# Re-pacing loads, crossbar transposes and attention units in a fused attention and bilinear feed-forward kernel

## The chip, the cores and the metric

The kernel runs on one core of a Trainium2 chip. The metric is the device time of one execution in microseconds (us). The profile's span, from the first to the last instruction, is about 2 us shorter. TensorE does the matrix products, ScalarE (ACT) and VectorE (DVE) empty the accumulators, GpSimd (POOL) copies, and issues the loads from memory. The SyncE queue (SPq) issues crossbar transposes and stores.

## The reference

For each of 4 batches and 8 heads, the sequence of 768 is cut into 8 blocks of 96. A Sinkhorn-normalised 8x8 matrix P mixes the blocks of k and v; attention is taken inside each block; and the result goes through a bilinear feed-forward network.

```python
k_sorted = einsum('bhij,bhjcd->bhicd', P, k_blocks)      # v likewise
attn     = softmax(scale * q_blocks @ k_sorted^T)         # inside each block
x        = (attn @ v_sorted)  as  [4*768, 512]
out      = ((x @ w_a) * (x @ w_b)) @ w_out                # 512 -> 1536 -> 512
```

## The kernel before

Heads are taken in pairs: batch 0 has pairs 0 to 3, batch 1 has 4 to 7, and so on. While TensorE computes the feed-forward products of batch b, the attention "units" of batch b+1 are put in between the products. A pair has three units: mix (k and v by P), scores (q times k, then exp), and o (weights times v). Three values per pair go through a crossbar transpose on the SyncE queue: q (tile `qTf`), mixed v (tile `vs`), and the o stage's result (`xp` to `xT`). `xT` is what the next batch's products read.

```python
def c_(g):                      # mix unit of pair g
    if g == HP: stage_q(g)
    if g + 1 < B * HP: stage_q(g + 1)          # transpose of a later q
    if g + 2 < B * HP: pair_q(g + 2)           # GpSimd copy ahead of it
    if g + HP < B * HP: load_pair((g + HP) // HP, g % HP)   # loads, one batch ahead
    stage_mix(g, "k", ("act",))
    stage_mix(g, "v", ("dve", "act"))          # ends in the transpose to vs
def o_(g):
    stage_o(g)                                 # o_ps <- vs, eT ; xp on DVE
    to_xT(g)                                   # transpose xp -> xT
# units of a batch: c4, sc4, c5, o4, sc5, c6, o5, sc6, c7, o6, sc7, o7
# interleave: one unit every so many steps; a step is a product pair (ffn_ab) or an output product (ffn_out)
...
# before batch 1 starts, on the GpSimd queue:
for hp in range(2): load_pair(1, hp)           # two pairs of batch 1
spread(nc.gpsimd, p_col, 8, 8)                 # 2 us
for c in range(3): load_out(c)                 # w_out
pair_q(HP); pair_q(HP + 1)
for hp in range(2, HP): load_pair(1, hp)       # the other two pairs
```

In the profile, `pf` and `two` are the accumulators of ffn_ab (x times w_a or w_b), and `po` that of ffn_out (one step is 12 matmuls). `mix`, `sc` and `o_ps` are the units.

The softmax here doesn't subtract the row's maximum and nothing guards it: scores larger than these inputs give would overflow.

Of the kernel before, what the change touches and what calls it, by code (L numbers as in the profile page):

```python
# [10 lines left out]
BF16 = mybir.dt.bfloat16  # L11
# [5 lines left out]
def _ap(t: bass.AP, extra_offset, pattern):  # L17
    return bass.AP(tensor=t.tensor, offset=t.offset + extra_offset,
                   ap=[list(p) for p in pattern])
# [3 lines left out]
def kernel(  # L23
# [11 lines left out]
    nc = tc.nc  # L35
    P = 128
    B, H, S, D = q.shape
    NB = sort_net.shape[-1]
# [7 lines left out]
    NCH = S // P  # L46
    HP = H // 2
    KA = DMODEL // P
    KO = DFF // P
# [11 lines left out]
    const = ctx.enter_context(tc.tile_pool(name="const", bufs=1))  # L61
    ld = ctx.enter_context(tc.tile_pool(name="ld", bufs=8))
    qtp = ctx.enter_context(tc.tile_pool(name="qtp", bufs=5))
# [23 lines left out]
    def load_pair(b, hp):  # L87
        tiles = []
        for name, t in (("k2", k), ("v2", v), ("q2", q)):
            base = (b * H + 2 * hp) * S * D  # L90
            if b == 0 and name == "q2":
                continue
            to = ld.tile([P, 2, W], BF16, tag=name, name=name)
            nc.gpsimd.dma_start(out=to, in_=_ap(t, base, [[W, P], [S * D, 2], [1, W]]))  # L94
            tiles.append(to)
        loaded[b * HP + hp] = tiles
# [43 lines left out]
    st = {}  # L140
    xTs = {}

    def xT_of(b):
        if b not in xTs:
            xTs[b] = xtp.tile([P, KA, S], BF16, tag="xT", name="xT")
        return xTs[b]

    s_all = const.tile([P, BH, NB, CG], BF16, name="s_all")
    p_col = const.tile([P, NB, BH], BF16, name="p_col")

# [7 lines left out]
    def copy(eng, out, in_):  # L158
        if eng == "act":
            nc.scalar.copy(out=out, in_=in_)  # L160
        else:
            nc.vector.tensor_copy(out=out, in_=in_)  # L162
# [89 lines left out]


    def pair_q(g):
        qc = qtp.tile([P, NCH, 2, D], BF16, tag="qc", name="qc", bufs=3)
        nc.gpsimd.tensor_copy(out=qc.rearrange("p c e d -> p e c d"),  # L256
                              in_=loaded[g][2].rearrange("p e (c d) -> p e c d", c=NCH))
        st[g, "qc"] = qc

    def stage_q(g):  # L260
        qT = qtp.tile([P, NCH, P], BF16, tag="qTf", name="qTf", bufs=3)
        nc.sync.dma_start_transpose(out=qT, in_=st[g, "qc"].rearrange("p c e d -> p (c e d)"))
        st[g, "qT"] = qT

# [21 lines left out]
    def stage_scores(g):  # L286
        kT, qT, eT = kTs[g % NBUF], st[g, "qT"], eTs[g % NBUF]
        for hf in range(2):
            sc = psA.tile([P, 2, 512], FP32, tag="A", name="sc")
            for i in range(NBH):  # L290
                for e in range(2):
                    blk = hf * NBH + i
                    nc.tensor.matmul(  # L293
                        sc[:, e, i * BLK:(i + 1) * BLK],
                        lhsT=kT[e * D:(e + 1) * D, blk * BLK:blk * BLK + P],
                        rhs=qT[e * D:(e + 1) * D, :, blk * CG:(blk + 1) * CG],
                        start=True, stop=True)
            nc.scalar.activation(out=eT[:, hf, :, 0:HB], in_=sc[0:BLK, :, 0:HB],  # L298
                                 func=AF.Exp, scale=float(scale))
# [7 lines left out]
    def to_xT(g):  # L307
        xT, xp = xT_of(g // HP), st[g, "xp"]
        nc.sync.dma_start_transpose(
            out=xT[:, g % HP, :].rearrange("p (i t) -> p i t", i=NB),  # L310
            in_=xp.rearrange("p i e d -> p (i e d)"))
# [9 lines left out]
    def ab_mms(pf, w_sb, b, m, t, kcs):  # L321
        for kc in kcs:
            nc.tensor.matmul(pf[:, 0:HW], lhsT=w_sb[:, kc, m * P:(m + 1) * P],  # L323
                             rhs=x_cols(b, kc, t), start=(kc == 0), stop=(kc == KA - 1))

    def hT_of(b):
        if b not in hTs:
            hTs[b] = ffp.tile([P, KO, S], BF16, tag="hT", name="hT")
        return hTs[b]

    def ffn_ab(b, m, t, begun=()):
        hT = hT_of(b)
        ab = []
        for n, w_sb in enumerate((w_a_sb, w_b_sb)):
            if n < len(begun):
                pf, k0 = begun[n], KA - 1
            else:
                pf, k0 = psF.tile([P, 512], FP32, tag="F", name="pf"), 0
            ab_mms(pf, w_sb, b, m, t, range(k0, KA))
            ab.append(pf)  # L340
            if n == 0:
                a_sb = ffp.tile([P, HW], BF16, tag="a_sb", name="a_sb", bufs=4)
                nc.scalar.copy(out=a_sb, in_=pf[:, 0:HW])  # L343
        nc.vector.tensor_mul(out=hT[:, m, t * HW:(t + 1) * HW], in0=a_sb,  # L344
                             in1=ab[1][:, 0:HW])

    def ffn_out(b, c):
        hT = hTs[b]
        po = psF.tile([P, DMODEL], FP32, tag="F", name="po")
        for m in range(KO):  # L350
            nc.tensor.matmul(po, lhsT=hT[:, m, c * P:(c + 1) * P], rhs=w_out_sb[:, m, :],  # L351
                             start=(m == 0), stop=(m == KO - 1))
        o_sb = ffp.tile([P, DMODEL], FP32, tag="o_sb", name="o_sb", bufs=3)
        copy("act" if c % 2 == 0 else "dve", o_sb, po)
        if b == 0:
            h, u = divmod(c, 3)
            for c2 in range(2):
                nc.sync.dma_start(
                    out=_ap(out, (h * PH * NCH + 2 * u + c2) * DMODEL,
                            [[NCH * DMODEL, PH], [1, DMODEL]]),  # L360
                    in_=o_sb[c2 * PH:(c2 + 1) * PH])
        else:
            rows = out[b * S:(b + 1) * S, :].rearrange("(p c) n -> c p n", c=NCH)
            nc.sync.dma_start(out=rows[c], in_=o_sb)


    with tc.manual_schedule(engines={ET.PE, ET.Pool, ET.SP}):
        with tc.manual_schedule(engines={ET.Activation, ET.DVE}):
# [4 lines left out]
            for it in range(5):  # L373
                nc.scalar.activation(out=p_nat, in_=p_nat, func=AF.Exp)  # L374
                if it == 2:
                    with nc.allow_low_precision("sum of one one and zeros"):
                        nc.vector.reduce_sum(
                            out=mask, in_=_ap(ident, 0, [[P, P], [1, CG], [CG, NB]]),
# [10 lines left out]
                else:  # L389
                    nc.vector.tensor_mul(  # L390
                        out=p_fin.bitcast(BF16).rearrange("h (i j u) -> h i j u", i=NB, j=NB),
# [69 lines left out]

        for c in range(4, 6):
            load_ab(c)
        for hp in range(2):
            load_pair(1, hp)
        spread(nc.gpsimd, p_col, 8, 8)
        for c in range(3):
            load_out(c)
        pair_q(HP)
        pair_q(HP + 1)  # L470
        for hp in range(2, HP):
            load_pair(1, hp)
        for g in range(2, 4):
            spread(nc.gpsimd, p_col, g * 8, 8)

# [25 lines left out]
        def units_full(b):  # L501
            g0, us = b * HP, []

            def c_(g):
                if g == HP:
                    stage_q(g)
                if g + 1 < B * HP:
                    stage_q(g + 1)
                if g + 2 < B * HP:
                    pair_q(g + 2)  # L510
                if g + HP < B * HP:
                    load_pair((g + HP) // HP, g % HP)
                stage_mix(g, "k", ("act",))
                stage_mix(g, "v", ("dve", "act"))

            def o_(g):
                stage_o(g)
                to_xT(g)

            for n in range(HP + 1):  # L520
                if n < HP:
                    us.append(lambda g=g0 + n: c_(g))
                if n > 0:
                    us.append(lambda g=g0 + n - 1: o_(g))
                if n < HP:
                    us.append(lambda g=g0 + n: stage_scores(g))
            return us

        def interleave(steps, units, spare, slow=0):
            n, done = len(steps), 0  # L530
            for s, step in enumerate(steps):
                step()
                want = s + 1 if s < slow else -(-(s + 1) * len(units) // (n - spare))
                while done < min(want, len(units)):
                    units[done]()
                    done += 1

        steps = [lambda: ffn_ab(0, 0, 0, begun[0:2]), lambda: ffn_ab(0, 1, 0, begun[2:4]),
                 lambda: ffn_ab(0, 2, 0, begun[4:5])]
        steps += [lambda m=m: ffn_ab(0, m, 0) for m in range(3, KO)]  # L540
        interleave(steps, units_half(), 1, 3)

        steps = [lambda m=m: ffn_ab(0, m, 1) for m in range(KO)]
        steps += [lambda c=c: ffn_out(0, c) for c in range(NCH)]
        interleave(steps, units_full(1), 2)

        for b in range(1, B):
            steps = [lambda m=m, t=t, b=b: ffn_ab(b, m, t)
                     for m in range(KO) for t in range(2)]
            steps += [lambda c=c, b=b: ffn_out(b, c) for c in range(NCH)]  # L550
            interleave(steps, units_full(b + 1) if b + 1 < B else [], 2)


# [28 lines left out]
```

## Time and profile before

| before | value |
|---|---|
| time, median | 256.2 us (3 runs, 253.7 to 257.0) |
| span of the profiled run | 252.7 us |
| TensorE busy | 234.4 us |
| mean granted TensorE clock | 0.993 |
| TensorE waits for transposes | 5.4 us |

The page's first part has, for each engine, busy microseconds, share of the span, and instruction count.

```profile
PE 234.4 (93%) x2219; PEld 135.6 (54%) x2229; DVE 108.2 (43%) x259; ACT 102.4 (41%) x202; POOL 61.4 (24%) x83
```

TensorE is idle for 18.3 us. The list of TensorE's waits (who waited for what: total us, times, longest) says what can be removed.

```profile
PE q_ps L175 <- DMA q_first<-in_q_dram: 6.2, 1, 6.2
PE o_ps L241 <- DMA vs<-vT: 5.4, 2, 3.3
PE o_ps L241 <- ACT eT L210: 0.6, 1, 0.6
```

The first line is the start. The second is two waits for a transposed v. The table of stretches (window and length, then busy time of each engine, then the granted clock, DMA share and GB/s) shows that everything removable is in one stretch, the time of batch 0's second half beside batch 1's attention.

```profile
45.00:92.70 47.70, 42.01 (x397) 23.30 (x399) 17.27 (x37) 18.63 (x36) 20.49 (x26) 0.96 1.36 180
92.70:147.40 54.70, 54.60 (x489) 31.42 (x489) 23.10 (x47) 23.91 (x47) 7.47 (x10) 1.00 0.59 108
147.40:202.00 54.60, 54.49 (x488) 31.50 (x489) 23.06 (x47) 23.91 (x47) 0.00 (x0) 1.00 0.34 74
```

The timeline of TensorE (start, length, instruction, count; in brackets the idle time before it and what ended it) shows the second wait and its cost afterwards.

```profile
76.44 1.04 PE L241 MATMUL o_ps<-vs,eT 96*128 96x65 bf16 x16 [3.33 <-DMA vs<-vT]
77.29 4.02 PE L351 MATMUL po<-w_out_sb,hT 128*128 128x512 bf16 x12
81.25 0.52 PE L293 MATMUL sc<-qTf,kT 64*128 64x96 bf16 x16
81.69 2.76 PE L351 MATMUL po<-w_out_sb,hT 128*128 128x512 bf16 x11
```

Twelve matmuls take 4.02 us right after the idle time; eleven take 2.76 us a little later. The granted clock between 77.5 and 79.5 us is 0.50.

Why is v late? The view of DMA issues gives us from issue to landing. The first line here is the v transpose issued at 63.4 us, in the crowded stretch; the second is the transpose to xT issued at 129.8 us, with no load beside it.

```profile
vs<-vT SPq DMA_TRANSPOSE x1, 12.9
xT<-xp SPq DMA_TRANSPOSE x1, 2.8
```

### The profile page before, as it was taken

The page shows a single profiled execution, that of the slowest core. Times are in us where ns is not written, and L with a number is a line of the kernel's source. Part 1 is how long each engine was busy: PE and PEld are TensorE (multiplying, and loading weights), DVE is VectorE, ACT ScalarE, POOL GpSimd, SP SyncE. Part 2 cuts the span into 40 slices and gives each one's busy share as a digit, 9 for nine tenths or more (in the row PEclk, how much of TensorE's full clock was granted, in tenths as well). Part 3 has the DMA queues.
Part 4 walks back from the last instruction along what each step waited for, and adds up shares of the span by engine and source line. Part 5 has one row for each costly group of instructions (what it writes and reads, how often), then busy time and mean ns, then how long its engine had stood idle before and what let it go on. Part 6 is the DMA issues. An engine that isn't in the chain of part 4 may idle for free.

```text
span 252.7 us, 5448 instructions
## 1 busy us (share of the span) xinstructions
PE 234.4 (93%) x2219; PEld 135.6 (54%) x2229; DVE 108.2 (43%) x259; ACT 102.4 (41%) x202; POOL 61.4 (24%) x83
## 2 busy tenths in 40 slices
PE   0999899969958999999999999999999999999993
PEld 0475566536624455666654456666654466665441
DVE  6775456535613313555453133645533144444111
ACT  3385555556520217463740137465440033333010
POOL 8974678554715305300100000000000000000000
PEclk9999999999997999999999999999999999999999
DMA  6999999999999998992332343332244210000122
GB/s 88 197 199 196 197 200 201 190 169 184 146 129 199 239 204 160 160 116 45 72 65 83 115 118 73 67 74 40 42 35 125 113 44 0 0 0 4 52 114 83
DMA packets 56441, 28.67 MB, mean 113 GB/s; under 512 B 33376, under 2 KB 53344, under 8 KB 56416
## 3 DMA queue, kind: packets, MB, share of 16 engines
q0 software_dynamic: 20944, 14.16, 40.6%
q1 hardware_dynamic: 35472, 14.17, 28.9%
q8 instruction: 17, 0.28, 0.4%
q14 instruction: 8, 0.07, 0.1%
HBM read 28.32 MB, written 6.29 MB: 137 GB/s over the span
## 4 chain that ended last, share of the span: by engine, by line
PE 83%; DMA 9%; DVE 5%; ACT 1%; issue 1%; DVEq 0%
PE pf L323 46%; PE po L351 24%; DMA vs<-vT 8%; PE o_ps L241 3%; PE mix L272 3%; PE sc L293 2%; PE mixh L191 2%; PE vs_ps L218 1%; PE sc L206 1%; PE xt_ps L232 1%; DMA p_nat<-in_sort_net_dram 1%; DVE hT L344 1%; DVE xph L247 1%; DVE csum L384 1%; ACT p_nat L374 1%
## 5 line engine op out<-in xcount | busy, mean ns | idle before, releaser
L344 DVE TENSOR_TENSOR hT<-a_sb,pf 128x384 bf16<-128x384 bf16 x95 | 52.6, 554 | 74.0 <-PE pf L323 45.5
L323 PE MATMUL pf<-xT,w_a_sb 128*128 128x384 bf16 x380 | 78.1, 327 | 0.0
L323 PE MATMUL pf<-xT,w_b_sb 128*128 128x384 bf16 x380 | 77.5, 326 | 0.0
L343 ACT CAST a_sb<-pf 128x384 bf16<-128x384 f32 x95 | 45.5, 479 | 65.9 <-PE pf L323 49.4
L351 PE MATMUL po<-w_out_sb,hT 128*128 128x512 bf16 x279 | 64.5, 385 | 0.5
L323 PEld LDWEIGHTS <-w_b_sb 128*128 128x128 bf16 x384 | 37.5, 98 | 25.1 <-issue 0.6
L323 PEld LDWEIGHTS <-w_a_sb 128*128 128x128 bf16 x384 | 34.6, 98 | 22.1
L351 PEld LDWEIGHTS <-hT 128*128 128x128 bf16 x288 | 28.0, 99 | 33.3 <-issue 1.6
L162 DVE COPY o_sb<-po 128x512 f32<-128x512 f32 x12 | 8.3, 692 | 47.8 <-PE po L351 31.3
L160 ACT COPY o_sb<-po 128x512 f32<-128x512 f32 x12 | 7.0, 586 | 43.0 <-PE po L351 23.1
L298 ACT ACTIVATE eT<-sc 96x768 bf16<-96x768 f32 x24 | 18.1, 802 | 12.4 <-PE sc L293 12.4
L256 POOL COPY qc<-q 128x768 bf16<-128x768 bf16 x12 | 9.9, 826 | 53.1 <-DMA qTf<-qc 34.0
L241 PE MATMUL o_ps<-vs,eT 96*128 96x65 bf16 x256 | 11.6, 196 | 6.1 <-DMA vs<-vT 5.4
L247 DVE TENSOR_TENSOR xp<-o_ps,rec 96x512 bf16<-96x512 f32 x24 | 15.5, 680 | 0.3
L241 PEld LDWEIGHTS <-eT 96*128 96x128 bf16 x256 | 10.5, 99 | 8.9 <-issue 6.3
L160 ACT CAST kT<-mix 128x384 bf16<-128x384 f32 x24 | 10.3, 482 | 6.2 <-PE mix L272 6.2
L94 POOL DMA_DIRECT2D v<-in_v_dram x16 | 11.5, 718 | 1.8 <-DMA w_b_sb<-in_moe_w_b_dram 0.8
L94 POOL DMA_DIRECT2D k<-in_k_dram x16 | 11.5, 719 | 1.2 <-DMA w_a_sb<-in_moe_w_a_dram 0.6
L245 DVE RECIPROCAL rec<-o_ps 96x8 f32<-96x8 f32 x32 | 5.2, 185 | 12.1 <-PE o_ps L241 12.0
L94 POOL DMA_DIRECT2D q<-in_q_dram x12 | 8.6, 719 | 1.3 <-DMA w_a_sb<-in_moe_w_a_dram 0.7
L175 PE MATMUL q_ps<-ident,q_first 64*64 64x64 bf16 x96 | 3.0, 217 | 6.2 <-DMA q_first<-in_q_dram 6.2
L210 ACT ACTIVATE eT<-sc 96x768 bf16<-96x768 f32 x8 | 6.5, 808 | 2.5 <-PE sc L206 2.5
(69 smaller groups left out, 138.4 us busy)
## 6 DMA issues: line engine op xcount, KB each, us to landing
out_dram<-o_sb SPq DMA_DIRECT2D x18, 256.0 KB, 2.0
k<-in_k_dram POOLq DMA_DIRECT2D x16, 192.0 KB, 6.4
v<-in_v_dram POOLq DMA_DIRECT2D x16, 192.0 KB, 6.8
q<-in_q_dram POOLq DMA_DIRECT2D x12, 192.0 KB, 9.1
w_a_sb<-in_moe_w_a_dram POOLq DMA_DIRECT2D x6, 256.0 KB, 10.8
w_b_sb<-in_moe_w_b_dram POOLq DMA_DIRECT2D x6, 256.0 KB, 10.7
w_out_sb<-in_moe_w_out_dram POOLq DMA_DIRECT2D x3, 512.0 KB, 10.9
out_dram<-o_sb SPq DMA_DIRECT2D x12, 128.0 KB, 5.1
```

Of the source, the lines that this page charges most:

```text
L94: nc.gpsimd.dma_start(out=to, in_=_ap(t, base, [[W, P], [S * D, 2], [1, W]]))
L160: nc.scalar.copy(out=out, in_=in_)
L162: nc.vector.tensor_copy(out=out, in_=in_)
L241: nc.tensor.matmul(o_ps[:, e, i * (D + 1):(i + 1) * (D + 1)], lhsT=eT[:, hf, e, i * BLK:i * BLK + P], rhs=vs[0:BLK, i0 + i, V0 - 1 + e * ( ...
L247: nc.vector.tensor_tensor(out=_ap(xp, i0 * 2 * D, [[nxp * 2 * D, BLK], [D, 2], [2 * D, NBH], [1, D]]), in0=_ap(o_ps, 1, [[1024, BLK], [511 ...
L256: nc.gpsimd.tensor_copy(out=qc.rearrange("p c e d -> p e c d"), in_=loaded[g][2].rearrange("p e (c d) -> p e c d", c=NCH))
L272: nc.tensor.matmul(mix[e * D:(e + 1) * D, c // 3, c % 3 * P:(c % 3 + 1) * P], lhsT=src2[:, e, c * D:(c + 1) * D], rhs=s_all[:, 2 * g + e], ...
L298: nc.scalar.activation(out=eT[:, hf, :, 0:HB], in_=sc[0:BLK, :, 0:HB], func=AF.Exp, scale=float(scale))
L323: nc.tensor.matmul(pf[:, 0:HW], lhsT=w_sb[:, kc, m * P:(m + 1) * P], rhs=x_cols(b, kc, t), start=(kc == 0), stop=(kc == KA - 1))
L343: nc.scalar.copy(out=a_sb, in_=pf[:, 0:HW])
L344: nc.vector.tensor_mul(out=hT[:, m, t * HW:(t + 1) * HW], in0=a_sb, in1=ab[1][:, 0:HW])
L351: nc.tensor.matmul(po, lhsT=hT[:, m, c * P:(c + 1) * P], rhs=w_out_sb[:, m, :], start=(m == 0), stop=(m == KO - 1))
```

## The change

The intent is to keep loads out of the way of transposes and to give each transpose more time. It has three parts:

- **L**, load order. All of batch 1's loads are issued first, then w_out, then all four q copies and their transposes.
- **G**, gate. A later batch's loads move from the mix unit to the o stage, after a one-element GpSimd copy that reads the o stage's result `xp`. So GpSimd can't issue them before that o stage is done. The later q copies and transposes move with them.
- **U**, units. The order becomes mix, scores, o of the pair before, so a v transpose has five units' time instead of four. Units are spread by TensorE time, an ffn_out step counting as two ffn_ab steps.

```diff
 # L
-        for hp in range(2):
+        for hp in range(HP):
             load_pair(1, hp)
         spread(nc.gpsimd, p_col, 8, 8)
         for c in range(3):
             load_out(c)
-        pair_q(HP)
-        pair_q(HP + 1)
-        for hp in range(2, HP):
-            load_pair(1, hp)
+        for g in range(HP, 2 * HP):
+            pair_q(g)
+            stage_q(g)
 # G
             def c_(g):
-                ... stage_q(g + 1), pair_q(g + 2), load_pair((g + HP) // HP, g % HP)
                 stage_mix(g, "k", ("act",))
                 stage_mix(g, "v", ("dve", "act"))
             def o_(g):
                 stage_o(g)
                 to_xT(g)
+                if 2 * HP <= g + 2 < B * HP:
+                    pair_q(g + 2)
+                    stage_q(g + 2)
+                if g + HP < B * HP:
+                    nc.gpsimd.tensor_copy(out=gate, in_=st[g, "xp"][0:1, NB - 1, 1, D - 1:D])
+                    load_pair((g + HP) // HP, g % HP)
 # U
                 if n < HP:
                     us.append(lambda g=g0 + n: c_(g))
+                    us.append(lambda g=g0 + n: stage_scores(g))
                 if n > 0:
                     us.append(lambda g=g0 + n - 1: o_(g))
-                if n < HP:
-                    us.append(lambda g=g0 + n: stage_scores(g))
+        def paced(ab, po, units, spare):
+            steps = [(1, f) for f in ab] + [(2, f) for f in po]
+            total = sum(t for t, f in steps) - 2 * spare
+            ...                       # runs a unit while done * total < now * len(units)
 # cuts: the two q tiles get 4 buffers instead of 3; the calls of interleave are replaced
```

After the last o stage two ffn_out steps are left in batch 0 and three in the others; it was three and four.

More of the change, by code (lines that the diff above doesn't have):

```diff
@@ L146, in xT_of @@
         return xTs[b]
+    gate = const.tile([1, 1], BF16, name="gate")
     s_all = const.tile([P, BH, NB, CG], BF16, name="s_all")
@@ L254, in pair_q @@
     def pair_q(g):
-        qc = qtp.tile([P, NCH, 2, D], BF16, tag="qc", name="qc", bufs=3)
+        qc = qtp.tile([P, NCH, 2, D], BF16, tag="qc", name="qc", bufs=4)
         nc.gpsimd.tensor_copy(out=qc.rearrange("p c e d -> p e c d"),
@@ L260, in stage_q @@
     def stage_q(g):
-        qT = qtp.tile([P, NCH, P], BF16, tag="qTf", name="qTf", bufs=3)
+        qT = qtp.tile([P, NCH, P], BF16, tag="qTf", name="qTf", bufs=4)
         nc.sync.dma_start_transpose(out=qT, in_=st[g, "qc"].rearrange("p c e d -> p (c e d)"))
@@ L504, in c_ @@
             def c_(g):
-                if g == HP:
-                    stage_q(g)
-                if g + 1 < B * HP:
-                    stage_q(g + 1)
-                if g + 2 < B * HP:
-                    pair_q(g + 2)
-                if g + HP < B * HP:
-                    load_pair((g + HP) // HP, g % HP)
                 stage_mix(g, "k", ("act",))
@@ L536, in interleave @@
                     done += 1
+        def paced(ab, po, units, spare):
+            steps = [(1, f) for f in ab] + [(2, f) for f in po]
+            total = sum(t for t, f in steps) - 2 * spare
+            now = done = 0
+            for t, step in steps:
+                step()
+                now += t
+                while done < len(units) and done * total < now * len(units):
+                    units[done]()
+                    done += 1
         steps = [lambda: ffn_ab(0, 0, 0, begun[0:2]), lambda: ffn_ab(0, 1, 0, begun[2:4]),
@@ L541 @@
         interleave(steps, units_half(), 1, 3)
-        steps = [lambda m=m: ffn_ab(0, m, 1) for m in range(KO)]
-        steps += [lambda c=c: ffn_out(0, c) for c in range(NCH)]
-        interleave(steps, units_full(1), 2)
-        for b in range(1, B):
-            steps = [lambda m=m, t=t, b=b: ffn_ab(b, m, t)
-                     for m in range(KO) for t in range(2)]
-            steps += [lambda c=c, b=b: ffn_out(b, c) for c in range(NCH)]
-            interleave(steps, units_full(b + 1) if b + 1 < B else [], 2)
+        for b in range(B):
+            ab = [lambda m=m, t=t, b=b: ffn_ab(b, m, t)
+                  for m in range(KO) for t in range(2) if b > 0 or t == 1]
+            po = [lambda c=c, b=b: ffn_out(b, c) for c in range(NCH)]
+            paced(ab, po, units_full(b + 1) if b + 1 < B else [], 2)
 _INS = ['q', 'k', 'v', 'sort_net', 'moe_w_a', 'moe_w_b', 'moe_w_out']
```

## The prediction

> **What bounds it now.** TensorE: 234.4 of 252.7 us busy (page, part 1). In the table of stretches it is idle 0.1 of 46.8 us in 92.7-139.5 and 0.1 of 46.6 us in 147.4-194: nothing to gain there. Of its 18.3 us idle, 6.2 are the start and 4 the tail, both untouched; the rest stands between 45 and 77 us: the list of waits shows two TensorE waits for the crossbar-transposed v (o_ps for vs), 2.12 us at 57.1 and 3.33 us at 76.4, 5.45 us together. After the second the granted clock is 0.50 until about 80 us: the next 12 po matmuls take 4.02 us instead of 2.65, o_ps 1.04 instead of 0.65, 1.76 us more. This fits the Trainium skill, "TensorE: Matmul & The Clock Gate", Part 1, where an idle window of about 3.4 us halves the clock; the 2.12 us stall left it at 1.00. Removable: about 7.2 us.
>
> **Why the stalls.** Transposes that land in 2.8-3.3 us in the quieter stage (94-130 us) take 7.6-12.9 us in 49-77 us (DMA view), beside loads of batch 1 issued at 39.8-43.2 and of batch 2 at 53-70. The vs that stalls longest: issued 63.4, landed 76.3. The skill's "DMA: Bandwidth & Descriptors", "Issuing engines are not separate DMA queues", says all issuers share 16 engines and interleave; the trace agrees.
>
> **What changes.** TensorE executes the same instructions, reordered. Batch 1's twelve loads are issued together, w_out after them, then four pair_q copies (0.82 us each) and their transposes. Loads of batch 2 start only after the first full o stage (about 60 us instead of 53). A vs gets five units instead of four: in this stage about 9-11 us instead of 7. Both old stalls should go: -7 us.
>
> **What comes back.**
> 1. The first full pair's q transpose was issued at 36.9 and landed 9.7 us later, at 46.6, before its scores at 49.5. Now it stands behind six more loads, a 2.0 us spread and w_out on GpSimd: issued at about 43, with some 8 us of loads still queued, landing at about 51-53. Estimate: a new stall of 2 us (0-4).
> 2. Batch 1's last o stage is followed by 2 po (5.3 us) instead of 3 (7.9). Before, the last xT landed 8.2 us after that stage and only just sufficed. Loads gated by the preceding o stage collide with it. Estimate: 1.5 us (0-4) before batch 1's first product finishes, at kc = 3.
> 3. Later batches keep three po there: nothing.
>
> Sum: -7.2 +2 +1.5 = -3.7 us on a median of 256.2: **252.5 us**, range 248.7 to 256.2. Faster by over 2%: 0.34; within 2%: 0.62; slower by over 2%: 0.04.
>
> **What would show it.** Right: no o_ps wait for vs; vs landings of 3-6 us in 50-85 us; clock 1.0 at 77-80 us; TensorE busy about 232.5 us; first batch-2 load at about 60 us. The first scores waiting for qTf near 50 us, and the product after the last po of batch 0 waiting for xT near 90 us, would show items 1 and 2.
>
> **What would make it wrong.** If the q transposes overtake the queued loads and xT lands sooner without them, all 7 us come through: 249, faster. If the first vs queues behind four q transposes until past its o stage (about 60 us), or a new stall is long enough to halve the clock again, the gain is gone: 255-256.

## The result, and the profile after

| | before | after |
|---|---|---|
| time, median | 256.6 us (4 runs, 253.7 to 262.2) | 270.5 us (4 runs, 269.3 to 271.4) |
| span, profiled run | 252.7 | 268.1 |
| TensorE busy | 234.4 | 237.9 |
| mean granted clock | 0.993 | 0.967 |

The ratio is 1.058, with a 95% interval of 1.047 to 1.069. Ratios here are the mean time of one kernel's fast runs over that of the other's fast runs of the same rounds, so they are not quite the ratio of the medians. The runs of before vary between rounds and chips (medians of 256.3 to 259.6 us), so kernels are compared by ratio.

The change made the kernel 5.8% slower; 1.4% faster was predicted (252.5 on 256.2). The page's first part, after:

```profile
PE 237.9 (89%) x2217; PEld 137.3 (51%) x2229; DVE 109.2 (41%) x259; ACT 102.5 (38%) x202; POOL 63.1 (24%) x91
```

TensorE's idle time grew from 18.3 to 30.2 us (268.1 - 237.9), and its busy time by 3.5 us for the same matmuls. Those two make up the whole 15.4 us of span. The list of waits names the idle time:

```profile
PE pf L324 <- DMA xT<-xp: 10.6, 2, 6.4
PE sc L294 <- DMA qTf<-qc: 5.7, 2, 4.7
PE o_ps L242 <- DMA vs<-vT: 0.2, 1, 0.2
```

The old waits for v are gone, as intended. In their place products wait for xT at the starts of batches 1 and 2, and scores wait for q. The timeline of TensorE shows the three longest and the slow clock after each:

```profile
55.05 0.83 PE L294 MATMUL sc<-qTf,kT 64*128 64x96 bf16 x16 [4.68 <-DMA qTf<-qc]
55.81 1.46 PE L324 MATMUL pf<-xT,w_a_sb 128*128 128x384 bf16 x4
...
99.79 0.48 PE L324 MATMUL pf<-xT,w_a_sb 128*128 128x384 bf16 x1 [6.37 <-DMA xT<-xp]
100.06 1.48 PE L324 MATMUL pf<-xT,w_b_sb 128*128 128x384 bf16 x4
...
161.56 0.40 PE L324 MATMUL pf<-xT,w_a_sb 128*128 128x384 bf16 x1 [4.20 <-DMA xT<-xp]
161.75 1.49 PE L324 MATMUL pf<-xT,w_b_sb 128*128 128x384 bf16 x4
...
165.48 0.81 PE L324 MATMUL pf<-xT,w_b_sb 128*128 128x384 bf16 x4
```

Four pf matmuls take 0.81 us at full clock, and 1.46 to 1.49 us after a stall. The table of stretches shows the cost by place; the two short rows are the starts of batches 1 and 2.

```profile
45.00:93.40 48.40, 43.13 (x405) 24.04 (x408) 18.12 (x39) 18.75 (x36) 15.66 (x21) 0.93 0.90 131
93.40:104.00 10.60, 4.23 (x35) 2.41 (x34) 1.43 (x3) 1.74 (x4) 0.82 (x1) 0.68 1.13 191
104.00:157.30 53.30, 52.08 (x453) 29.85 (x455) 21.73 (x45) 22.17 (x44) 11.67 (x19) 1.00 0.66 94
157.30:166.00 8.70, 4.50 (x38) 2.60 (x37) 1.78 (x3) 2.05 (x5) 1.64 (x2) 0.80 0.85 187
166.00:217.20 51.20, 51.04 (x448) 29.33 (x450) 21.72 (x44) 21.82 (x43) 0.00 (x0) 1.00 0.30 70
```

Why is xT late? First the SyncE queue and then GpSimd, at the end of batch 0 (same columns as the timeline). The transpose of 89.94 us is the one that TensorE waits for until 99.79.

```profile
85.86 1.24 SPq L310 DMA_TRANSPOSE xT<-xp  x1
87.20 1.36 SPq L263 DMA_TRANSPOSE qTf<-qc  x1
88.65 1.20 SPq L359 DMA_DIRECT2D out_dram<-o_sb  x2
89.94 2.02 SPq L310 DMA_TRANSPOSE xT<-xp  x1
```

```profile
85.96 0.18 POOL L515 COPY gate<-xp 1x1 bf16<-1x1 bf16 x1 [5.91 <-DVE xp L248]
86.47 0.72 POOL L94 DMA_DIRECT2D k<-in_k_dram  x1 [0.34 <-issue]
...
90.14 0.18 POOL L515 COPY gate<-xp 1x1 bf16<-1x1 bf16 x1
90.27 0.72 POOL L94 DMA_DIRECT2D k<-in_k_dram  x1
```

The gate opens when `xp` is written, and the transpose of `xp` is issued at that same moment (85.86 beside 85.96, 89.94 beside 90.14). So each pair's three loads start together with that pair's transpose. At the end of a batch the two last o stages are one ffn_out step apart, so six loads are near the last transpose. It lands after 9.8 us here, and after 9.9 us at the end of batch 1. In the middle of batch 1, where only the three loads of its own stage are beside it, it takes 4.5 to 5.2 us. The view of DMA issues for the transpose of 89.94 us:

```profile
xT<-xp SPq DMA_TRANSPOSE x1, 9.8
```

The first wait is another matter. On GpSimd, the q copies now stand behind six more loads, the spread and w_out. The transpose of the first q is issued at 43.45 us (36.88 before) and lands 11.5 us later (9.7 before), at about 54.9. The SyncE queue, the first line from before and the second from after, and then the landing in after:

```profile
36.88 4.25 SPq L262 DMA_TRANSPOSE qTf<-qc  x2
43.45 11.53 SPq L263 DMA_TRANSPOSE qTf<-qc  x4
```

```profile
qTf<-qc SPq DMA_TRANSPOSE x1, 11.5
```

### The profile page after: what moved, and what is told of

Read it like the earlier page. It is cut to its first block, busy times and chain, and to the rows that moved or that the text cites. A ratio compares the mean times of both kernels' runs of the same rounds, so it can differ in the third digit from the quotient of the medians.

```text
span 268.1 us, 5456 instructions
## 1 busy us (share of the span) xinstructions
PE 237.9 (89%) x2217; PEld 137.3 (51%) x2229; DVE 109.2 (41%) x259; ACT 102.5 (38%) x202; POOL 63.1 (24%) x91
## 4 chain that ended last, share of the span: by engine, by line
PE 64%; DMA 27%; POOL 5%; issue 2%; DVE 1%; SPq 1%; POOLq 0%; DVEq 0%
PE pf L324 39%; PE po L352 18%; DMA xT<-xp 7%; DMA qTf<-qc 7%; DMA w_b_sb<-in_moe_w_b_dram 4%; DMA v<-in_v_dram 4%; PE mix L273 3%; DMA vs<-vT 3%; DMA k<-in_k_dram 2%; PE sc L294 2%; PE o_ps L242 2%; POOL w_out_sb L110 1%; POOL s_all L153 1%; POOL q_first L82 1%; POOL w_a_sb L105 1%
## 5 line engine op out<-in xcount | busy, mean ns | idle before, releaser
L324 PE MATMUL pf<-xT,w_a_sb 128*128 128x384 bf16 x380 | 80.1, 333 | 10.6 <-DMA xT<-xp 10.6
L324 PE MATMUL pf<-xT,w_b_sb 128*128 128x384 bf16 x380 | 79.4, 332 | 0.0
L352 PE MATMUL po<-w_out_sb,hT 128*128 128x512 bf16 x277 | 63.2, 379 | 0.7 <-issue 0.2
L324 PEld LDWEIGHTS <-w_a_sb 128*128 128x128 bf16 x384 | 35.4, 99 | 23.7 <-issue 1.9
L352 PEld LDWEIGHTS <-hT 128*128 128x128 bf16 x288 | 27.4, 98 | 31.4
L299 ACT ACTIVATE eT<-sc 96x768 bf16<-96x768 f32 x24 | 18.1, 803 | 11.3 <-PE sc L294 11.3
L515 POOL COPY gate<-xp 1x1 bf16<-1x1 bf16 x8 | 1.4, 180 | 72.9 <-DVE xp L248 72.9
L94 POOL DMA_DIRECT2D k<-in_k_dram x16 | 11.5, 719 | 4.2 <-issue 1.3
L94 POOL DMA_DIRECT2D v<-in_v_dram x16 | 11.5, 717 | 3.6 <-DMA w_b_sb<-in_moe_w_b_dram 2.0
L294 PE MATMUL sc<-qTf,kT 64*128 64x96 bf16 x192 | 6.5, 210 | 5.7 <-DMA qTf<-qc 5.7
L294 PEld LDWEIGHTS <-kT 64*128 64x128 bf16 x192 | 4.7, 97 | 10.0 <-issue 7.3
```

The lines of the kernel that those rows point to most:

```text
L94: nc.gpsimd.dma_start(out=to, in_=_ap(t, base, [[W, P], [S * D, 2], [1, W]]))
L294: nc.tensor.matmul(sc[:, e, i * BLK:(i + 1) * BLK], lhsT=kT[e * D:(e + 1) * D, blk * BLK:blk * BLK + P], rhs=qT[e * D:(e + 1) * D, :, blk ...
L299: nc.scalar.activation(out=eT[:, hf, :, 0:HB], in_=sc[0:BLK, :, 0:HB], func=AF.Exp, scale=float(scale))
L324: nc.tensor.matmul(pf[:, 0:HW], lhsT=w_sb[:, kc, m * P:(m + 1) * P], rhs=x_cols(b, kc, t), start=(kc == 0), stop=(kc == KA - 1))
L352: nc.tensor.matmul(po, lhsT=hT[:, m, c * P:(c + 1) * P], rhs=w_out_sb[:, m, :], start=(m == 0), stop=(m == KO - 1))
```

## The experiments

Two causes were supposed, each with a rival. For xT: theory A, the gate's collision of loads with the transpose; rival B, that the pacing leaves too few products after the last o stage. For q: theory C, its place on the GpSimd queue; rival D, that transposes are slow there whatever their place. In the kernels with parts switched off, the q tiles keep their four buffers. All runs gave correct results.

| run | parts | wait for qTf | for xT | for vs | median us | ratio to before (95%) |
|---|---|---|---|---|---|---|
| before | none | 0 | 0 | 5.4 | 256.6 | 1 |
| after | L G U | 5.7 | 10.6 | 0.2 | 270.5 | 1.058 (1.047-1.069) |
| e3_LU | L U | 4.8 | 3.5 | 2.2 | 263.3 | 1.031 (1.017-1.046) |
| e6_LG | L G | 5.0 | 0 | 0 | 255.0 | 1.004 (0.992-1.016) |
| e2_GU | G U | 1.0 | 11.4 | 0 | 263.1 | 1.033 (1.016-1.050) |
| e4_U_again | U | 0 | 4.1 * | 6.2 * | 259.3 | 1.011 (1.003-1.018) |
| e5_G | G | 0 | 1.3 | 2.0 | 251.4 | 0.980 (0.971-0.988) |
| e7_LG_qfirst | L G, q first | 0 * | 4.0 * | 3.0 * | 254.5 | 0.995 (0.987-1.004) |
| e10_qfirst | L G U, q first | 0.6 * | 10.6 * | 0 * | 265.5 | 1.038 (1.030-1.046) |
| e11_old_order | L G, pacing of U | 2.1 | 2.2 | 0 | 259.7 | 1.014 (1.004-1.024) |
| e8_after_xT | L G U, last loads late | 5.6 | 0.5 | 0 | 255.8 | 1.002 (0.996-1.008) |
| e9_spare4 | L G U, 4 steps spare | 9.7 | 1.6 | 0 | 266.2 | 1.040 (1.032-1.047) |
| e12_both | L G U, both mends | 1.0 | 0.5 | 0 | 249.5 | 0.976 (0.970-0.983) |

Waits are those of the profiled run of each. A star marks a profile that fell in a slow run (over 1.5% above that kernel's fastest), so its waits are not an example of the fast runs.

### Parts switched off

**e3_LU**: without the gate.

```diff
 def c_(g):
+    if g + 1 >= 2 * HP and g + 1 < B * HP: stage_q(g + 1)
+    if g + 2 >= 2 * HP and g + 2 < B * HP: pair_q(g + 2)
+    if g + HP < B * HP: load_pair((g + HP) // HP, g % HP)
 def o_(g):
-    pair_q(g + 2); stage_q(g + 2); gate; load_pair(...)
```

> The changed kernel with its gate taken out: loads of later batches and the later q copies stand in the mix unit again, ungated, as before the change; load order and pacing stay new. Theory A (the gate releases a pair's loads at the moment its xT transpose is issued, so they share the DMA engines): the two waits of the product for xT (6.4 and 4.2 us in the changed kernel) go, with their slow-clock tails, 14 us less, about 256 us; the first scores still wait about 4.7 us for qTf. Rival B (pacing leaves too few products after the last o stage): the xT waits stay near 10 us and the time near 268 us.

The xT waits fell from 10.6 to 3.5 us, both parts of it now at the start of batch 1. At the end of batch 1 the last xT lands in 2.8 us, and there is no wait. But 256 us did not come: the time was 263.3. The 3.5 us for xT stayed, the ungated loads brought back a wait of 2.2 us for v, and the mean clock was still 0.974. Theory A holds for the start of batch 2. At the start of batch 1 the last xT took 7.5 us beside ungated loads. Before, one that took 6.6 us with one more product after it cost no wait, so the new pacing has a part in this one.

**e6_LG**: the old unit order and spread.

```diff
-    c_(n), stage_scores(n), o_(n-1)      # paced
+    c_(n), o_(n-1), stage_scores(n)      # interleave(ab + po, units, 2)
```

> The changed kernel with the old unit order and the old even spread over steps; load order and gate stay new. Theory A: xT waits remain at both batch starts, smaller by the one more product of 2.6 us that follows the last o stage: about 3.5 and 1.5 us instead of 6.4 and 4.2; total 262 to 266 us. Rival B: both xT waits under 0.5 us, total about 256 us. Under both the first scores still wait for qTf.

The xT waits are gone, which is what rival B said and theory A did not. The last xT of batch 1 lands in 4.7 us instead of 9.9, with the gate still there. So the gate alone does not do it; gate and unit order do it together. (The old spread also leaves one more product at the end; e11 below takes that out.) That is a third theory, E: the two last o stages stand one step apart and release their loads nearly at once.

**e2_GU**: the old load order.

```diff
-for hp in range(HP): load_pair(1, hp)
+for hp in range(2): load_pair(1, hp)
 spread; w_out
-four pair_q and stage_q
+pair_q(HP); pair_q(HP + 1); the other two pairs of loads   # stage_q in the mix units
```

> The changed kernel with the old initial order: two pairs of batch 1, w_out, two q copies and then the other two pairs. Theory C (the first q transposes come late because six more loads and w_out stand before them on the GpSimd queue): the wait of the first scores for qTf falls from 4.7 us to under 0.5 us, its slow-clock tail of 2 us goes, and the total is about 6.8 us less, 263.5 us; xT waits stay about 10 us. Rival D (the transposes are slow there whatever their place, because w_out or the loads fill the DMA engines): the wait stays over 2 us.

As theory C expected: the first scores no longer wait, and the time fell to 263.1 us (263.5 expected). The 1.0 us left is at 122.2 us, at scores of batch 2.

**e4_U** and **e4_U_again**: the kernel before with unit order and pacing alone (the diff's part U).

> The kernel before with only the new unit order and pacing (five units instead of four between a v transpose and its o stage); loads as before the change. If the old stalls come from too short a lead, the o_ps wait for vs falls from 5.45 us to under 3 us; xT waits at the start of batch 1 at most 3 us (one product fewer after the last o stage), none at the start of batch 2. Theory A: 252 to 256 us. Rival B: xT waits of about 10 us in all, over 262 us.

The profiled execution of e4_U took 1336 us, and its other three runs 256.8 to 262.4, so the ratio was unclear. In that one execution the products' matmuls were over four times as long (pf 1.35 to 1.38 us on average instead of 0.33, po 1.70 instead of 0.39), though the recorded mean clock was 1.0; VectorE and ScalarE kept theirs (0.55 us for the product into hT, 0.48 for the copy of pf). It says nothing about the change, and was not seen again in this kernel.

> The run of unit order and pacing alone again, since its profile fell into an execution of 1336 us and its ratio was unclear (1.016, 0.992 to 1.039). Expected from the runs without the gate: xT wait at the start of batch 1 of 2 to 4 us with its slow clock, none at the start of batch 2 where the last xT lands in 2.8 us; wait for vs under 3 us; 256 to 260 us.

The time was 259.3 us, slower than before by 1.1%. The profile is of the slow run of the four, so its waits (6.2 us for v, 4.1 for xT) are told without weight. What the times show is that U as a whole gains nothing without the other parts. U gives v more lead and leaves fewer products for xT, and how much each of the two did is not shown.

**e5_G**: the gate alone (the diff's part G).

> The kernel before with only the gate (loads and q copies of later batches in the o stages); load order, unit order and even spread as before. Theory A/E: with the old order the gate does no harm at the batch starts (xT waits under 1 us), and the old wait of 3.3 us for vs with its slow clock goes, because batch 2's loads no longer run beside it; the first wait for vs (2.1 us, beside batch 1's own loads) stays: about 251 to 254 us. If the gate alone were to blame: xT waits of 10 us, 265 us.

This is faster than before, 251.4 us, ratio 0.980. The longer of the two old waits for v is gone, one of 2.0 us stays, and there is an xT wait of 1.3 us: the last xT of batch 0 took 8.0 us, although in the old order the last two o stages stand two steps apart. The part that looked guilty in the trace of after is, by itself, the good part.

### The xT waits: collision, bunching or slack

**e11_old_order**: the changed kernel with the old unit order but the new pacing. The same two and three ffn_out steps follow the last o stage, but the o stage before it is now two steps away instead of one.

```diff
-    c_(n), stage_scores(n), o_(n-1)
+    c_(n), o_(n-1), stage_scores(n)      # still paced
```

> The changed kernel with the old order of units (mix, o of the pair before, scores) but the new pacing. The last o stage still has two and three products after it, but the o stage before it is two products away instead of one. Theory E (two o stages close together release six gated loads at once into the last xT): landings of the last xT fall from 9.8 us to 5 to 7 us, waits for xT from 10.6 to 2 to 4 us, total about 259 us. Rival B (only the number of products left counts): waits stay 9 to 11 us, total about 269 us.

The last xT landed in 6.1 us (batch 0's end) and 4.9 us (batch 1's), instead of 9.8 and 9.9. The waits fell to 2.2 us with the number of products left unchanged. So B alone does not hold. E holds clearly at batch 1's end: there the runs with the gate and the old order have 4.7 to 5.1 us (e5, e6, e7, e11), and those with the gate and U 9.6 to 10.1 (after, e2, e9, e10). At batch 0's end it is less clear: 6.1 to 6.3 us (e11, e6), but 8.0 (e5) and 10.6 (e7, a slow run), against 8.7 to 10.5 with U. So something besides the distance of the o stages has a part there, and it stays open. The time of 259.7 us was as expected; the profiled run was the fastest of the four, at 257.4.

**e9_spare4**: the pacing ends two products earlier; the o stages stay one step apart.

```diff
-            paced(ab, po, units_full(b + 1) if b + 1 < B else [], 2)
+            paced(ab, po, units_full(b + 1) if b + 1 < B else [], 4)
```

> The changed kernel with the pacing ending two products earlier (four and five products after the last o stage instead of two and three), the two last o stages still one product apart, loads still gated by them. Slack alone: the last xT still lands in 9 to 10 us, but the product now comes 10.6 and 13 us after the o stage, so the waits fall from 6.4 and 4.2 us to about 1 and 0 us; the first scores still wait 4.7 us; total 257 to 260 us. If the landing grew with more stores beside it, waits of over 3 us would stay.

The last xT still took 10.5 and 10.1 us, and the wait for it fell to 1.6 us as expected. But the time was 266.2 us, not 257 to 260. Others waited instead: scores for q 9.7 us in all, 5 us more than the first scores' 4.65, and one product waited 2.9 us for an accumulator whose output copy was held up by the stores. The two new q waits (2.73 and 2.32 us, in the middle of batch 1) are not from slower transposes: these landed in 7.1 and 6.7 us (6.7 and 6.1 in after), but with the units closer together the scores were ready 4.4 us after the issue, where the one of after that waited (1.06 us) was ready 5.7 us after it. The slack at the end was taken from the spacing of the units, and the wait moved there.

**e8_after_xT**: the loads of a batch's last two pairs wait until that batch's last xT has landed. Nothing else is changed: unit order, pacing, stores and q transposes stand where they did.

```diff
-    if g + HP < B * HP:
+    if g + HP < B * HP and g % HP < HP - 2:
         gate on st[g, "xp"]; load_pair((g + HP) // HP, g % HP)
+    if g + HP < B * HP and g % HP == HP - 1:
+        nc.gpsimd.tensor_copy(out=gate, in_=xT_of(g // HP)[0:1, HP - 1, S - 1:S])
+        load_pair((g + HP) // HP, HP - 2)
+        load_pair((g + HP) // HP, HP - 1)
```

> The changed kernel, unit order and pacing kept, but a batch's last two pairs of loads are gated on the landing of that batch's last xT transpose instead of on their own o stages, so that none of them is in flight beside it. Theory A (the collision with gated loads makes the last xT take 9.8 and 9.9 us): it lands in 3 to 6 us, the waits for xT fall from 10.6 us to under 1 us, total about 256 us (the first scores still wait 4.7 us). Rival B2 (the stores and the q transpose on the same DMA queue delay it): landings stay over 7 us, waits over 6 us.

TensorE's waits in this run:

```profile
PE sc L294 <- DMA qTf<-qc: 5.6, 2, 4.5
PE o_ps L242 <- ACT eT L211: 0.6, 1, 0.6
PE pc_ps L413 <- POOL p_rep L407: 0.6, 1, 0.6
PE pf L324 <- DMA xT<-xp: 0.5, 1, 0.5
```

The SyncE queue at the end of batch 0, to be read beside that of after, and the landing of its last xT:

```profile
86.98 1.24 SPq L263 DMA_TRANSPOSE qTf<-qc  x1
88.31 2.08 SPq L359 DMA_DIRECT2D out_dram<-o_sb  x2
90.48 1.28 SPq L310 DMA_TRANSPOSE xT<-xp  x1
```

```profile
xT<-xp SPq DMA_TRANSPOSE x1, 2.8
```

The same q transpose and the same two stores stand ahead of it, and it lands in 2.8 us instead of 9.8 (2.8 instead of 9.9 at batch 1's end). Only the loads beside it were taken away. So the loads were the cause, and rival B2 (stores and q transposes) falls. The time is 255.8 us, as expected.

### The q wait: place on the queue

**e10_qfirst** (in the changed kernel) and **e7_LG_qfirst** (in e6_LG): two q copies and transposes go ahead of the spread and w_out.

```diff
 for hp in range(HP): load_pair(1, hp)
+for g in range(HP, HP + 2): pair_q(g); stage_q(g)
 spread(nc.gpsimd, p_col, 8, 8)
 for c in range(3): load_out(c)
-for g in range(HP, 2 * HP): pair_q(g); stage_q(g)
+for g in range(HP + 2, 2 * HP): pair_q(g); stage_q(g)
```

> The changed kernel with only the first two q copies and transposes moved ahead of the mask spread and w_out. Theory C: the first scores' wait falls from 4.7 us to under 0.5 us, its slow clock goes, xT waits stay about 10 us: total about 263 us. Rival D: that wait stays over 2 us, total over 266 us.

> New load order and gate with the old unit order and spread (the run whose xT waits were 0), and now the first two q copies and their transposes stand before the mask spread and w_out on the GpSimd queue. Theory C (place on the queue): the first q transpose is issued near 38.5 us instead of 43, lands before 49 us, the wait of 5.0 us and its slow clock of 2 us go, total 247 to 249 us, faster than the kernel before by 2.5 to 3.5%. Rival D (transposes take as long as w_out and the loads are moving, whatever their place): still over 2 us of wait, 251 us or more.

In both, the first q transpose was issued at 38.9 us and landed after 7.2 to 7.3 us, before its scores at about 50, so they no longer waited. Both profiles are of slow runs; the same is seen in the fast profile of e12_both below. e10 took 265.5 us, near the 263 expected. e7 was a miss: 254.5 us instead of 247 to 249. Its profile shows the first v transposed beside w_out, landing after 8.5 us and waited for 3.0 us, where e6_LG, held up by the scores, had v land in 3.1 us. The 4.0 us for xT in it (landing after 10.6 us at batch 0's end) belong to the slow run, and how much of them its fast runs have is open.

### Both mends together

**e12_both**: the edits of e8_after_xT and e10_qfirst in the changed kernel, all of L, G and U kept.

> The changed kernel with both mends: the first two q copies and transposes ahead of the mask spread and w_out, and a batch's last two pairs of loads gated on the landing of its last xT. Unit order and pacing as changed. If the two causes are the whole loss and add up, all waits of the product for xT and of the scores for qTf stay under 1 us, the clock at 0.99 or more, span 246 to 248 us, time about 249 us, ratio to the kernel before 0.965 to 0.975. If something else is lost in the new pacing: over 252 us.

The page's first part and clock row, and then the waits:

```profile
PE 232.3 (94%) x2217; PEld 134.8 (55%) x2229; DVE 108.6 (44%) x259; ACT 102.1 (41%) x202; POOL 63.1 (26%) x89
...
PEclk9999999999999999999999999999999999999999
```

```profile
PE q_ps L176 <- DMA q_first<-in_q_dram: 6.3, 1, 6.3
PE sc L294 <- DMA qTf<-qc: 1.0, 1, 1.0
...
PE pf L324 <- DMA xT<-xp: 0.5, 1, 0.5
```

The span is 247.2 us, the mean clock 1.000, the time 249.5 us. The ratio to before is 0.976 (0.970 to 0.983): faster than before, though the interval does not lie wholly beyond 2%. So with both causes mended the loss is gone; the 1.0 us for q is at scores of batch 2, at 113.7 us. Here the extra lead of U does help: the first v again takes 8.4 us to land, and nothing waits for it. But e5_G, the gate alone, reached 0.980 (0.971 to 0.988) in the same rounds. That L and U, mended, add anything to the gate is therefore not shown.

## Why the prediction was wrong, point by point

The same matmuls take 232.3 us at full clock (e12_both, clock 1.000). Against that, the slow clock cost 2.1 us before (234.4 - 232.3) and 5.6 us after (237.9 - 232.3).

| term of the sum | predicted | measured, in the span |
|---|---|---|
| old waits for v go | -5.45 | -5.2 |
| the slow clock after the old stall goes | -1.76 | -2.1 |
| new wait for q | +2 | +5.7 (4.68 and 1.06) |
| xT at the start of batch 1 | +1.5 | +6.37 |
| xT at the start of batch 2 | 0 | +4.20 |
| slow clock after the new stalls | not counted | +5.6 |
| sum | -3.7 | +14.6 of the 15.4 seen |

- **Right:** what bounded the kernel, where the 7.2 us lay, that the old waits go, and that nothing is to be had in the later batches. In after itself there was luck in it: the q wait held back the first o stage too, which gave its v more time. That the wait also goes without this is shown by e12_both.
- **Mis-sized, mechanism right:** "Estimate: a new stall of 2 us (0-4)" for the q transpose. It was issued at 43.45 us (43 predicted) and landed at 54.9 instead of 51 to 53. The step that failed is its landing time: it took 11.5 us, more than the 8 us of queued loads. e10_qfirst (issued at 38.9 us, landed after 7.2) and e2_GU show that the place on the queue is the cause.
- **Mis-sized, with a part missing:** "Estimate: 1.5 us (0-4) before batch 1's first product finishes, at kc = 3". The place was right to the matmul (the fourth, kc = 3). But the prediction reckoned from before's 8.2 us between that o stage and the landing of xT, 6.6 of them the transpose's own. Here it was 12.0 us (87.75 to about 99.7), 9.8 of them the transpose's own. That loads "gated by the preceding o stage collide with it" was said. That the o stage's own loads start with it too, and that the new order puts the two o stages one step apart, was missed.
- **The step that failed outright:** "Later batches keep three po there: nothing." The only landings that the prediction names there, 2.8 to 3.3 us at 94 to 130 us, are those of transposes with no loads beside them: before, batch 3's loads were all issued by about 103 us. Three transposes in that same stretch, issued at 102.75, 107.90 and 109.22 us, took 8.9, 4.5 and 3.8 us, and the prediction passed over them. The gate spreads batch 3's loads over the o stages beside batch 1's products, down to the last. So the collision of batch 0's end came again at batch 1's end, 4.20 us. The change's own effect on that stage was left out.
- **Left out of the sum:** the slow clock after new stalls. It was counted as a gain for the old stall, and named at the end as a danger, but no new stall was charged with it, as the two expected (2 and 1.5 us) were shorter than the one of before that left the clock at 1.00 (2.12 us). Three new stalls of over 4 us cost 5.6 us.

The Trainium skill, "DMA: Bandwidth & Descriptors", section "Issuing engines are not separate DMA queues", says that transfers of all issuers run on the same 16 engines and interleave. The runs agree: moving loads issued by GpSimd took the landing of a transpose issued by SyncE from 9.8 to 2.8 us. The skill's "TensorE: Matmul & The Clock Gate", Part 1, says that an idle window of about 3.4 us halves the clock; in after, waits of 4.20 to 6.37 us did so all three times (for shorter gaps, see the last section).

What is open: the fast runs of e7 were profiled in none, so where their time goes is inferred only. And that the loads delay the last xT is shown (e8), but not how. At batch 1's end of after the queues moved 203 GB/s throughout its 9.9 us; at batch 0's end 1.2 of the 9.8 us (91.2 to 92.4) passed at 9 GB/s, and no run says what held the transfers then.

## What to carry to other kernels

A gate should be placed by what it releases: a gate on the event that also starts an urgent transfer puts the two side by side, and a gate on that transfer's landing keeps them apart. When a change moves transfers to another stage, transfer times read in that stage before the change no longer hold, and any new stall long enough to slow the clock costs its tail too. More slack in one place is taken from the spacing in another, so take the competing transfers away first.

## What the Trainium skill lacked or had wrong

- "DMA: Bandwidth & Descriptors", section "DMA Transpose (X-bar)", gives no time from issue to landing of a transpose beside loads. Here xT (192 KB) took 2.8 us with none beside it, 4.5 to 5.2 us with the three loads of its own stage (middle of batch 1 of after), and 8.7 to 10.5 us with the six of two o stages one step apart; a q transpose among many queued loads took 11.5 us.
- The same page, "Issuing engines are not separate DMA queues", calls the time a sequencer needs to start a DMA usually small beside the DMA. For transposes in a crowd this case differs: four of them held the SyncE queue for 11.53 us from 43.45 us on, where one takes about 1.2 us in the quiet stages, and the first v transpose (its input was written by 50.1 us) stood behind them until 55.0 us.
- "TensorE: Matmul & The Clock Gate", Part 1, puts the idle window at about 3.4 us. Here shorter gaps slowed the clock too, and their length alone did not decide it: gaps of 1.95 us (e5_G, at 57.4 us), 2.11 (e11_old_order, 55.7), 2.91 (e9_spare4, 101.7) and 3.33 (before, 76.4) were followed by a granted clock of 0.53, 0.70, 0.59 and 0.50 over the next 3.3 us; gaps of 2.12 (before, 57.1), 2.25 (e3_LU, 68.6), 2.32 and 2.73 us (e9_spare4, 140.6 and 127.1) by 1.00. So no safe length between 1.95 and 2.9 us comes out of these runs.
- The same page reports a clock stuck at a quarter for over 50 us. One execution here (e4_U, 1336 us) had pf matmuls of 1.35 to 1.38 us on average instead of 0.33 from end to end, with a recorded mean clock of 1.0. The page warns that the clock records can be wrong; it has no case of a whole execution.
